# Attention's small matmuls in float32 as four tiles side by side, and the last weight's pages in the order of the products

## The chip, the cores and the metric

The kernel runs on one core of one Trainium2 chip. The metric is the device time of one execution in microseconds (us). The core has five engines that run their own instruction streams and wait for one another by semaphores: PE (TensorE, the matmuls, with its weight loads shown apart as PEld), DVE (VectorE), ACT (ScalarE), POOL (GpSimd) and SP (SyncE, which issues nearly all the DMAs here). Matmuls write PSUM, everything else lives in SBUF or DRAM.

## The reference

Attention over a small state, in both directions, and then two feed-forward blocks. All arrays are float32, except the four weight matrices, which arrive as float64.

```
x: [8, 8, 512, 64] (batch, head, position, 64)   state: [8, 8, 32, 64]
scores  = x @ state^T / 8        -> softmax over the 32 states   -> xread = a  @ state
scores2 = state @ x^T / 8        -> softmax over the 512 positions -> sread = a2 @ x
t = concat(xread, sread) as [4352 tokens, 512]
h = relu(t @ w_in)^2   @ w_out          (512 -> 2048 -> 512)
out = silu(h @ w2_in)  @ w2_out         (512 -> 2048 -> 512)
```

## The kernel before

**Precision.** The large matmuls are made of three products of one-pass float32 operands ("fp32r"): an operand is split into a high part (an ACT cast) and a low part (a subtraction on DVE or POOL), and high*high, high*low and low*high are summed in PSUM. A matmul on plain float32 operands shows as two MATMUL records and two LDWEIGHTS records in the trace.

**Attention.** It is done for a pair (b, g): batch b and a group g of four heads, so 16 pairs. `scores` fills one PSUM bank [4 heads x 32 states, 512 positions] from `x` (two halves l of 128 rows, two heads of 64 rows each). So that two heads of one half don't mix, the weights are a block form of the state, with zeros elsewhere. For the first three batches (b < NB = 3) the block form is a float32 quad `sblkf[b]`, filled by `s_put`, and each half is one float32 matmul of 128 rows, 128 columns and 512 moving columns. For the other five batches the block form (`sblk`, two pages, filled by `s_build`) and x (`x_split`) are split, and there are six one-pass matmuls. From the scores, DVE and ACT make both softmaxes. For the second direction `a2_T` transposes the softmax (four transposes on PE into PSUM), `a2_split` splits it on its way out of PSUM, `xn_split` splits x in its other layout, and `sread` makes 12 one-pass matmuls: 128 weight columns (4 heads x 32 states) against 256 moving columns (4 heads x 64), of which only the four diagonal blocks [32 x 64] are used; `sread_evac` takes those out. Scores, transposes and sread share the two PSUM banks `psD`.

**The first block.** `g_unit` multiplies the state with w_in once per batch pair (tile matmuls of 64 rows by 64 columns, with `tile_position`, weights from `st`, moving operand `cc`, into `psA` and `psB`). For batch j and each of 16 chunks c of the hidden width, `gemm1` multiplies the attention weights with that (6 matmuls into `psC`), `chain_a` takes relu and square, and `gemm2` adds the product with w_out (12 matmuls into `psA` and `psB`). The weights are converted from float64 on DVE and ACT as they come (`c_bits` and others).

**The second block.** Each of its two matmuls is done in Strassen-Winograd form with seven products. `gemm3(u, pp)` does token part u (five parts) and width part pp (four parts), in the order of products SEQ = 1, 2, 6, 7, 5, 3, 4; `gemm4(q)` does token part q (nine parts) in the order SEQ4 = 1, 6, 2, 7, 5, 4, 3. For w2_out there are 28 pages, w4p[jj][i] for width part jj and product i (256 KB each); product i of gemm4 needs those of all four jj, and its own operands `g0i0` and `g0i1` (two DMAs of 512 KB for token part 0, `g_op`). In the last token part of gemm3 `w4_load(pp)` asks for the seven pages of jj = pp, ahead of `gemm3(4, pp)`.

**Order.** Nothing is issued as it is written: `Plan` records all operations, with their reads and writes, and then a list scheduler orders each engine's stream. It always takes the operation that can start earliest by its cost model, and of those the most urgent. A `page` (50 buffers) or a `quad` (10 buffers) is given out in the order in which its first user was recorded; a later one may go first only if enough are free for all those ahead of it. DMAs are issued by SP in the planner's order. Two accumulating matmuls on the same PSUM region are dependent in the plan, and regions are told apart by partitions and bank. `cost` gives a matmul with a `tile_position` a quarter of its time.

Of the kernel before, what the change touches and what calls it, by code (L numbers as in the profile page):

```python
# [27 lines left out]
class Plan:  # L28
# [78 lines left out]
    def cost(self, eng, method, writes, reads, args):  # L107
        size = 1
        for ap in writes + reads:
            n = 1  # L110
            for d in ap.shape[1:]:
                n *= d
            size = max(size, n)
        psum = any(self.tiles.get(ap.tensor.name, (0, 0, ""))[2] == "ps" for ap in writes + reads)
        if eng == "dma":
            n = 1
            for d in writes[0].shape:
                n *= d
            return n * 4 / 360
        if eng == "pe":  # L120
            n = 1
            for d in writes[0].shape[1:]:
                n *= d
            if method == "transpose":
                return 109
            share = 4 if args.get("tile_position") else 1
            return max(n / 2.4 + 13, 109) * (4 if args["rhs"].dtype == F32 else 1) / share
        if eng == "act":
            return (145 if psum else 190) + size / 1.2 + (93 if "accum_out" in args else 0)
        if eng == "pool":  # L130
            return 190 + dict(tensor_tensor=2.2, memset=0.8).get(method, 3.5) * size
        fast = method in ("tensor_scalar", "tensor_copy", "memset") and not psum
        return 157 + size / (1.92 if fast else 0.96)
# [243 lines left out]
def attn_moe_moe_kernel(  # L377
# [52 lines left out]
    def page(name, dt=F32R):  # L430
        return plan.tile(pages, [P, 1024], dt, "page", name)
# [44 lines left out]
    def at(s, phase, fn, *a):  # L476
        ev[(s, phase)].append((fn, a))
# [78 lines left out]


    st = plan.tile(pages, [P, 4, 4, 2, NS], F32, "page", "st")
    sblk = [page(f"sblk{i}") for i in range(2)]
    sblkf = [quad(f"sblkf{b}") for b in range(NB)]  # L560
    ident = plan.tile(const, [P, P], F32, "ident", "ident")
    srT = plan.tile(pages, [P, 4, B * NS], F32, "page", "srT")

    def st_of(b, r):
        return st[r * 64:(r + 1) * 64, b // 2, :, b % 2].rearrange("p (g l) n -> p g l n", l=2)

    def s_build(b, dst, a):

        v = dst.rearrange("p (s g a c) -> p s g a c", s=2, g=2, a=4)
        for r in range(2):  # L570
            ps = slice(r * 64, (r + 1) * 64)
            src = st_of(b, r)
            hi, lo = (v[ps, s][:, :, a, r * NS:(r + 1) * NS] for s in range(2))
            split_into(hi, lo, src)

    def s_put(b, dst, a):

        v = dst.rearrange("p (g a c) -> p g a c", g=2, a=4)
        for r in range(2):
            ps = slice(r * 64, (r + 1) * 64)  # L580
            copy(v[ps, :, a, r * NS:(r + 1) * NS], st_of(b, r))


    w1p, gp = {}, {}
# [47 lines left out]

    a_x, a_xn, a_S, a_e, a_2, a_U, at_p = {}, {}, {}, {}, {}, {}, {}

    def sblk_build(b):
        s_build(b, sblk[b % 2], slice(0, 4, 3))

    def x_load(b, g):
        lo = page(f"xTr{b}{g}", F32)
        D.dma_start(lo.rearrange("p (l t) -> p l t", l=2),  # L640
                          xT[b, g * 256:(g + 1) * 256, :].rearrange("(l p) t -> p l t", p=P))
        a_x[(b, g)] = lo

    def x_split(b, g):
        raw, a_x[(b, g)] = a_x[(b, g)], (page(f"xThi{b}{g}"), page(f"xTlo{b}{g}"))
        split_into(*a_x[(b, g)], raw)

    def scores(b, g):
        x = a_x.pop((b, g))
        t = att_tile()  # L650
        a_S[(b, g)] = t
        if b < NB:
            for l in range(2):
                c0 = (2 * g + l) * P
                T.matmul(out=t, lhsT=sblkf[b][:, c0:c0 + P], rhs=x[:, l * 512:(l + 1) * 512],
                         start=l == 0, stop=l == 1)
            return
        hi, lo = x
        pg = sblk[b % 2]
        n = 0  # L660
        for l in range(2):
            c0 = (2 * g + l) * P
            for so, xp in ((0, hi), (512, hi), (0, lo)):
                T.matmul(out=t, lhsT=pg[:, so + c0:so + c0 + P], rhs=xp[:, l * 512:(l + 1) * 512],
                                 start=n == 0, stop=n == 5)
                n += 1

    def sm_first(b, g, defer=False):
        t = a_S[(b, g)]
# [59 lines left out]
            T.transpose(t[:, k * P:(k + 1) * P], e[:, k * P:(k + 1) * P], ident)  # L729
        a_2[(b, g)] = t  # L730

    def a2_split(b, g):
        t = a_2[(b, g)].rearrange("p (k c) -> p k c", k=4)
        pg = page(f"a2{b}{g}")
        v = pg.rearrange("p (k s c) -> p k s c", k=4, s=2)
        A.copy(v[:, :, 0, :], t)
        V.tensor_tensor(out=v[:, :, 1, :], in0=t, in1=v[:, :, 0, :].bitcast(F32), op=ALU.subtract)
        a_2[(b, g)] = v

    def xn_load(b, g):  # L740
        lo = page(f"xnr{b}{g}", F32)
# [1 line left out]
                      xN[b, :, g * 256:(g + 1) * 256].rearrange("(k p) c -> p k c", p=P))  # L743
        a_xn[(b, g)] = lo

    def xn_split(b, g):
        raw, a_xn[(b, g)] = a_xn[(b, g)], (page(f"xnhi{b}{g}"), page(f"xnlo{b}{g}"))
        split_into(*a_xn[(b, g)], raw)

    def sread(b, g):  # L750

        hi, lo = a_xn.pop((b, g))
        v = a_2.pop((b, g))
        t = att_tile()
        o = t[:, 0:256]
        for k in range(4):
            xs = slice(k * 256, (k + 1) * 256)
            for i, (w, x) in enumerate(((0, hi), (1, hi), (0, lo))):
                T.matmul(out=o, lhsT=v[:, k, w, :], rhs=x[:, xs], start=k + i == 0, stop=k == 3 and i == 2)
        a_2[(b, g)] = t  # L760

    def sread_evac(b, g):
        t = a_2.pop((b, g))
        for h in range(4):
            for e in range(2):
                ps = (h % 2) * 64 + e * NS
                V.transpose(out=srT[ps:ps + NS, 2 * g + h // 2, b * NS:(b + 1) * NS],
                            in_=t[h * NS:(h + 1) * NS, h * 64 + e * NS:h * 64 + (e + 1) * NS])


    gact, acc, yq, y_part = {}, {}, {}, {}
# [154 lines left out]
        v = pg.rearrange("p (k s c) -> p s k c", s=2, k=2)  # L926
        return v[:, 0], v[:, 1]

    def w4_load(jj):

        w4p[jj] = {}
        for i in SEQ4:
            w4p[jj][i] = page(f"w4{jj}_{i}")
            lo = f32(w4_views(w4p[jj][i])[1])
            if SRC_B[i] in (11, 12, 21, 22):
                w4_quarter(jj, SRC_B[i], lo)
            else:
                D.dma_start(lo, w4s_d[(SRC_B[i], jj)].rearrange("p (k c) -> p k c", k=2))

    def w4_split(jj, i):  # L940
        hi, lo = w4_views(w4p[jj][i])
        split_into(hi, lo, f32(lo))

    def x_op(u, i):
# [97 lines left out]
    def gemm4(q):  # L1042
# [4 lines left out]
        def prod(i, bank, first, last):  # L1047
            if q == 0:
                for jj in range(4):
                    w4_split(jj, i)  # L1050
            for b in range(c):
                for k in range(8):
                    hi, lo = gop[(q, i)][k // 4]
                    w = w4p[k // 2][i][:, k % 2 * 512:(k % 2 + 1) * 512]
                    ks = slice(k % 4 * c * P + b * P, k % 4 * c * P + (b + 1) * P)
                    for m, (g, o) in enumerate(((hi, 0), (hi, 256), (lo, 0))):
                        T.matmul(out=bank[:, b * 256:(b + 1) * 256], lhsT=g[:, ks], rhs=w[:, o:o + 256],
                                 start=first and b + k + m == 0, stop=last and k == 7 and m == 2,
                                 skip_group_check=True)
# [40 lines left out]

    def sched_attention(b, g, s, defer=False):
        at(s - 4, "dma", x_load, b, g)
        if b >= NB:
            if g == 0:
                at(s, "vec", sblk_build, b)
            at(s, "vec", x_split, b, g)
        elif g == 0:
            at(s, "vec", s_put, b, sblkf[b], slice(0, 4, 3))
        at(s + 1, "pe", scores, b, g)
        at(s + 1, "vec", sm_first, b, g, defer)  # L1110
        at(s + 2, "vec", sm1_exp, b, g)
        at(s + 3, "vec", sm1_norm, b, g)
        at(s + 4, "vec", sm1_T, b, g)
        if not defer:
            sched_sread(b, g, s + 4)

    def sched_sread(b, g, s):
        at(s - 3, "dma", xn_load, b, g)
        at(s, "vec", sm2_norm, b, g)
        at(s + 1, "pe", a2_T, b, g)  # L1120
        at(s + 1, "vec", a2_split, b, g)
        at(s + 1, "vec", xn_split, b, g)
        at(s + 2, "pe", sread, b, g)
        at(s + 2, "vec", sread_evac, b, g)

    def init():
        for t in sblkf:
            G.memset(t, 0.0)
        for t in sblk[::-1]:
            G.memset(t.bitcast(F32), 0.0)  # L1130

    def load_st():
        D.dma_start(st, sT)
# [7 lines left out]
    def slot(b, c):  # L1141
        return place[(b, c)]

    at(-14, "vec", init)
    for i in range(NC // 2):
        q, p = divmod(i, 2)
        if q < PARTS[0][1] // 4:
# [9 lines left out]
            at(-12, "dma", load_st)  # L1157
        at(n, "pe", g_unit, 2 * i)
        at(n, "pe", g_unit, 2 * i + 1)
    at(-10, "vec", s_put, 0, sblkf[0], slice(0, 4, 3))  # L1160
    for g in range(2):
        at(-8 + g, "dma", x_load, 0, g)
        at(-6 + g, "pe", scores, 0, g)
# [75 lines left out]
    for u in range(NU):  # L1239
        for pp in range(4):  # L1240
# [2 lines left out]
                w3_build(pp + 2)  # L1243
            if u == 1:
                w4_sums(pp)
            if u + 1 == NU:
                if pp == 3:
                    g_op(0, 1)
                w4_load(pp)
            gemm3(u, pp)  # L1250
            if pp == 3:
                for i in (SEQ if u + 1 < NU else SEQ4[1:]):
                    if u + 1 < NU:
# [45 lines left out]
```

## Time and profile before

| | |
|---|---|
| median of 3 runs | 1397.41 us (1393.69 to 1398.91) |
| profiled execution | 1396.56 us |
| its span, first to last instruction | 1394.8 us |
| PE busy | 1350.0 us, 97% |
| PE weight loads | 1169.2 us, 84% |
| DVE / ACT / POOL busy | 1006.7 (72%) / 693.0 (50%) / 44.8 us (3%) |
| mean granted TensorE clock | 0.991 of full speed |
| DMA | 283.19 MB, mean 203 GB/s |

The profiled execution is 1.8 us longer than its span. A share of busy time is a mean over stages: PE is idle for 45 us in all, nearly all of that in the first 135 us, around 1045 us and at the seams of the last stage.

### The profile page before, as it was taken

What the parts mean: (1) busy time and instruction counts of PE and PEld (TensorE: products, weight loads), DVE (VectorE), ACT (ScalarE), POOL (GpSimd) and SP (SyncE); (2) the same over time, 40 slices, a digit from 0 to 9 for tenths busy, and PEclk for the clock granted to TensorE, in tenths of its full rate; (3) what the DMA queues carried; (4) which work ended last, traced back from release to release, by engine and by line L of the source; (5) the groups of instructions that cost most, each with busy time, mean ns of one, the idle gap of its engine ahead of it and who ended that gap; (6) DMA issues with size and microseconds to landing.
All of it is one profiled execution on the core that took longest, in us unless ns stands there. A gap on an engine that the chain in (4) does not pass through costs nothing. (4 is left out here: it accounts for less than half of the span.)

```text
span 1394.8 us, 21037 instructions
## 1 busy us (share of the span) xinstructions
PE 1350.0 (97%) x7820; PEld 1169.2 (84%) x7820; DVE 1006.7 (72%) x1524; ACT 693.0 (50%) x1070; POOL 44.8 (3%) x42
## 2 busy tenths in 40 slices
PE   5889999999999999999999999999999999999998
PEld 1557688888888888888988889998879999999998
DVE  7898598878888888885997768677876455444443
ACT  6765776556555555554743424245563343333331
POOL 1000001100000000000020000000010000000000
PEclk9999999999999999999999999999999999999999
DMA  8841844535454535452759758678897566655664
GB/s 308 313 178 63 296 155 129 165 122 166 152 168 125 176 118 162 138 191 73 256 190 355 276 209 285 216 242 295 303 345 242 197 212 227 209 178 188 196 189 113
DMA packets 206965, 283.19 MB, mean 203 GB/s; under 512 B 13456, under 2 KB 148112, under 8 KB 206864
## 3 DMA queue, kind: packets, MB, share of 16 engines
q1 hardware_dynamic: 206864, 281.86, 60.7%
q8 instruction: 61, 1.00, 0.3%
q14 instruction: 40, 0.33, 0.1%
HBM read 161.35 MB, written 116.26 MB: 199 GB/s over the span
## 5 line engine op out<-in xcount | busy, mean ns | idle before, releaser
L185 ACT ACTIVATE rg<-psC 128x512 f32<-128x512 f32 (+1 forms) x144 | 82.6, 574 | 197.4 <-PE psC L185 195.4
L185 DVE TENSOR_TENSOR gact<-rg,gact 128x512 fp32r<-128x512 f32 (+1 forms) x139 | 90.8, 655 | 20.4 <-ACT rg L185 14.6
L185 PE MATMUL psC<-AThi,Ghi 128*128 128x512 f32 x256 | 100.9, 400 | 2.3 <-ACT rg L185 2.0
L185 PE MATMUL psC<-AThi,Glo 128*128 128x512 f32 x256 | 101.2, 401 | 1.6 <-DVE Glo L185 1.6
L185 PE MATMUL psC<-ATlo,Ghi 128*128 128x512 f32 x256 | 100.5, 397 | 1.9 <-DVE ATlo L185 1.9
L185 ACT ACTIVATE gact<-rg 128x512 fp32r<-128x512 f32 (+1 forms) x144 | 87.7, 609 | 7.6 <-DMA g<-go 4.1
L185 DVE TENSOR_TENSOR rg<-rg 128x512 f32<-128x512 f32 (+1 forms) x66 | 43.7, 662 | 50.5 <-ACT rg L185 50.3
L185 PEld LDWEIGHTS psC<-AThi,Ghi 128*128 128x128 f32 x256 | 48.1, 188 | 15.7 <-ACT rg L185 2.4
L185 PEld LDWEIGHTS psC<-AThi,Glo 128*128 128x128 f32 x256 | 48.2, 188 | 14.6 <-issue 2.1
L185 PEld LDWEIGHTS psC<-ATlo,Ghi 128*128 128x128 f32 x256 | 48.3, 189 | 13.8 <-DVE ATlo L185 2.6
L185 ACT ACTIVATE r<-r 128x1024 f32<-128x1024 f32 (+2 forms) x20 | 18.6, 932 | 62.9 <-DVE r L185 52.7
L185 DVE TENSOR_SCALAR cv<-cv 128x1024 f32<-128x1024 f32 (+1 forms) x64 | 43.3, 685 | 8.0 <-ACT cv L185 7.7
L185 ACT ACTIVATE rg<-rg 128x512 f32<-128x512 f32 (+1 forms) x78 | 46.3, 594 | 0.0
L185 ACT ACTIVATE cv<-raw 128x512 f32<-128x512 f32 x64 | 40.6, 667 | 7.3 <-DMA raw<-in_w_dram 6.3
L185 DVE SCALAR_TENSOR_TENSOR cc<-raw,cv 128x512 int32<-128x512 int32 x64 | 41.8, 683 | 3.3 <-DMA g<-go 3.1
L185 DVE SCALAR_TENSOR_TENSOR cv<-raw,cv 128x512 f32<-128x512 uint32 x64 | 41.6, 683 | 0.2
L185 DVE TENSOR_TENSOR W<-psC,U 128x512 f32<-128x512 f32 (+2 forms) x40 | 24.1, 609 | 22.5 <-PE psC L185 22.2
L185 PE MATMUL psA<-cc,st 64*64 64x512 f32 x128 | 26.1, 687 | 14.6 <-DVE cc L185 14.6
L185 DVE TENSOR_TENSOR Glo<-Glo,Ghi 128x1024 fp32r<-128x1024 f32 x31 | 37.7, 1215 | 1.2 <-ACT Ghi L185 1.0
L185 ACT ACTIVATE W<-W 128x1024 f32<-128x1024 f32 (+2 forms) x20 | 18.7, 933 | 39.6 <-DVE W L185 35.7
L185 ACT ACTIVATE r<-psA 128x512 f32<-128x512 f32 (+2 forms) x40 | 20.7, 534 | 33.3 <-PE psA L185 25.6
L185 ACT CAST Ghi<-Glo 128x1024 fp32r<-128x1024 f32 x32 | 33.5, 1045 | 1.2 <-DMA Glo<-go 1.2
(1244 smaller groups left out, 4587.2 us busy)
## 6 DMA issues: line engine op xcount, KB each, us to landing
raw<-in_w_dram SPq DMA_DIRECT2D x64, 512.0 KB, 6.2
t<-s SPq DMA_DIRECT2D x36, 512.0 KB, 5.1
Glo<-g SPq DMA_DIRECT2D x96, 128.0 KB, 4.3
t<-r SPq DMA_DIRECT2D x24, 512.0 KB, 4.5
xTr<-in_xT_dram SPq DMA_DIRECT2D x16, 512.0 KB, 7.6
g<-go SPq DMA_DIRECT2D x16, 512.0 KB, 5.2
xnr<-in_xN_dram SPq DMA_DIRECT2D x16, 512.0 KB, 5.2
x<-yt SPq DMA_DIRECT2D x32, 256.0 KB, 4.1
```

The source lines that it names most:

```text
L185: lambda engine=engine, method=method, a=a, k=k: getattr(engine, method)(*a, **k)))
```

## The change

Scores of all batches take the state `st` and the loaded `x` as they are, in float32, as four tile matmuls of 64 rows and 32 columns, one for each head, at tile positions (0,0), (64,32), (0,64) and (64,96). Sread takes x and one float32 copy of the transposed softmax, as 16 tile matmuls of 128 rows, 32 weight columns and 64 moving columns: four k steps, and in each the four heads at column positions 0, 32, 64 and 96. The block forms, their memsets and copies, and the splits of x, of the other layout of x and of the softmax go. The planner's cost of a tile matmul is divided by the share of the array that it takes. The pages of w2_out are asked for in the order of the products, seven behind each `gemm3(4, pp)`.

```diff
-            share = 4 if args.get("tile_position") else 1
+            share = 128 * 128 // (reads[0].shape[0] * writes[0].shape[0]) if args.get("tile_position") else 1
...
-    sblk = [page(f"sblk{i}") for i in range(2)]
-    sblkf = [quad(f"sblkf{b}") for b in range(NB)]
...
     def scores(b, g):
         x = a_x.pop((b, g))
         t = att_tile()
         a_S[(b, g)] = t
-        if b < NB:
-            for l in range(2):
-                c0 = (2 * g + l) * P
-                T.matmul(out=t, lhsT=sblkf[b][:, c0:c0 + P], rhs=x[:, l * 512:(l + 1) * 512],
-                         start=l == 0, stop=l == 1)
-            return
-        hi, lo = x
-        pg = sblk[b % 2]
-        n = 0
         for l in range(2):
-            c0 = (2 * g + l) * P
-            for so, xp in ((0, hi), (512, hi), (0, lo)):
-                T.matmul(out=t, lhsT=pg[:, so + c0:so + c0 + P], rhs=xp[:, l * 512:(l + 1) * 512],
-                                 start=n == 0, stop=n == 5)
-                n += 1
+            for r in range(2):
+                h, ps = 2 * l + r, slice(r * 64, (r + 1) * 64)
+                T.matmul(out=t[h * NS:(h + 1) * NS], lhsT=st[ps, b // 2, 2 * g + l, b % 2],
+                         rhs=x[ps, l * 512:(l + 1) * 512], start=True, stop=True, tile_position=(r * 64, h * NS))
...
-    def a2_split(b, g):
-        t = a_2[(b, g)].rearrange("p (k c) -> p k c", k=4)
-        pg = page(f"a2{b}{g}")
-        v = pg.rearrange("p (k s c) -> p k s c", k=4, s=2)
-        A.copy(v[:, :, 0, :], t)
-        V.tensor_tensor(out=v[:, :, 1, :], in0=t, in1=v[:, :, 0, :].bitcast(F32), op=ALU.subtract)
-        a_2[(b, g)] = v
+    def a2_copy(b, g):
+        c = quad(f"a2{b}{g}")
+        copy(c, a_2[(b, g)])
+        a_2[(b, g)] = c
...
     def sread(b, g):
...
+        x, a = a_xn.pop((b, g)), a_2.pop((b, g))
         t = att_tile()
-        o = t[:, 0:256]
         for k in range(4):
-            xs = slice(k * 256, (k + 1) * 256)
-            for i, (w, x) in enumerate(((0, hi), (1, hi), (0, lo))):
-                T.matmul(out=o, lhsT=v[:, k, w, :], rhs=x[:, xs], start=k + i == 0, stop=k == 3 and i == 2)
+            for h in range(4):
+                T.matmul(out=t[h * NS:(h + 1) * NS, 0:64], lhsT=a[:, k * P + h * NS:k * P + (h + 1) * NS],
+                         rhs=x[:, k * 256 + h * 64:k * 256 + (h + 1) * 64], start=k == 0, stop=k == 3,
+                         tile_position=(0, h * NS))
...
-            if u + 1 == NU:
-                if pp == 3:
-                    g_op(0, 1)
-                w4_load(pp)
-            gemm3(u, pp)
+            if u + 1 == NU and pp == 3:
+                g_op(0, 1)
+            gemm3(u, pp)
+            if u + 1 == NU:
+                for i, jj in [(i, jj) for i in SEQ4 for jj in range(4)][7 * pp:7 * pp + 7]:
+                    w4_load(i, jj)
```

Also gone are `s_build`, `s_put`, `x_split`, `xn_split`, their places in the schedule, and `init` with its five memsets on POOL. `w4_load` now asks for one page.

## Rows read from the trace of the kernel before

**Rows 1.** By stretch: length, busy PE, PEld, DVE, ACT, POOL; clock, DMA share, GB/s.
```profile
15.00:45.00 30.00, 27.64 (x141) 7.74 (x134) 26.41 (x45) 22.65 (x43) 0.00 (x0) 0.94 0.84 284
45.00:75.00 30.00, 26.62 (x108) 19.74 (x106) 23.20 (x33) 21.80 (x36) 0.00 (x0) 1.00 0.94 343
75.00:135.00 60.00, 51.86 (x202) 40.01 (x203) 58.31 (x96) 31.68 (x57) 0.92 (x2) 0.91 0.28 103
...
160.00:700.00 540.00, 540.00 (x2676) 456.50 (x2675) 448.80 (x791) 317.11 (x534) 19.18 (x16) 1.00 0.49 157
...
1000.00:1030.00 30.00, 30.00 (x137) 24.66 (x136) 23.89 (x31) 14.91 (x23) 4.75 (x3) 1.00 0.99 331
...
1050.00:1060.00 10.00, 10.00 (x71) 10.00 (x71) 6.24 (x6) 3.19 (x4) 0.00 (x0) 0.80 0.78 276
```

**Rows 2.** Attention's matmuls on PE by form: count, busy us, mean ns of one.
```profile
L185 PE MATMUL psD<-xnhi,a 128*128 128x256 f32 x128 | 32.9, 280 | 0.0
...
L185 PE MATMUL psD<-xThi,sblk 128*128 128x512 f32 x40 | 15.7, 392 | 0.0
L185 PE MATMUL psD<-xTr,sblkf 128*128 128x512 f32 x24 | 13.2, 639 | 3.7 <-issue 2.4 <-ACT Sc L185 1.3
```

**Rows 3.** PE in order of time at 210 us, scores of a later batch.
```profile
210.77 0.39 PE L185 MATMUL psD<-xThi,sblk 128*128 128x512 f32 x1
211.00 0.39 PE L185 MATMUL psB<-gact,hi('w2', 6)_464 128*128 128x512 f32 x1
```

**Rows 4.** Busy time over 17 spacings between one-pass matmuls of sread.
```profile
233.83:235.86 2.04, 2.04 (x18) 1.00 0.31 100
```

**Rows 5.** PE in order of time at 23 us: 64x64 tiles around a full float32 matmul.
```profile
23.70 1.09 PE L185 MATMUL psA<-cc,st 64*64 64x512 f32 x8
24.61 1.04 PE L185 MATMUL psB<-cc,st 64*64 64x512 f32 x8
25.57 1.12 PE L185 MATMUL psD<-xTr,sblkf 128*128 128x512 f32 x2
26.63 1.09 PE L185 MATMUL psA<-cc,st 64*64 64x512 f32 x8
```

**Rows 6.** The weight loads of the same stretch, in order of time.
```profile
27.11 0.15 PEld L185 LDWEIGHTS psB<-cc,st 64*64 64x64 f32 x4 [0.28 <-issue]
27.54 0.15 PEld L185 LDWEIGHTS psB<-cc,st 64*64 64x64 f32 x4 [0.28 <-issue]
```

**Rows 7.** PE in order of time at 151 us: a full one-pass matmul among tiles.
```profile
151.45 0.50 PE L185 MATMUL psC<-AThi,Ghi 128*128 128x512 f32 x1
151.88 0.65 PE L185 MATMUL psB<-cc,st 64*64 64x512 f32 x2
```

**Rows 8.** PE in order of time at 229 us: transposes.
```profile
228.80 0.82 PE L185 MATMUL psD<-ident,e 128*128 128x128 f32 x6
...
229.70 0.27 PE L185 MATMUL psD<-ident,e 128*128 128x128 f32 x1
```

**Rows 9.** PE in order of time at 1045 us: the seam between gemm3 and gemm4.
```profile
1044.85 0.50 PE L185 MATMUL psC<-w,g050hi 128*128 128x256 f32 x2 [1.75 <-ACT g050hi L185]
1048.89 0.58 PE L185 MATMUL psD<-w,g070lo 128*128 128x256 f32 x1 [3.54 <-DVE g070lo L185]
```

**Rows 10.** SP's queue in order of time ahead of that seam.
```profile
1023.87 2.12 SPq L185 DMA_DIRECT2D w<-w4d  x2
1026.04 0.49 SPq L185 DMA_DIRECT2D g060lo<-t  x1
...
1034.31 1.41 SPq L185 DMA_DIRECT2D g050lo<-t  x1
```

**Rows 11.** A page of w2_out as a DMA: size, us to landing.
```profile
w<-w4s SPq DMA_DIRECT2D x16, 256.0 KB, 4.7
```

**Rows 12.** The splits of x for sread on ACT and DVE, ns min/median/max.
```profile
L185 ACT CAST xnhi<-xnr x16: 1032/1038/1064, 220.6 to 545.1; 128x1024 fp32r<-128x1024 f32 x16
L185 DVE TENSOR_TENSOR xnlo<-xnr,xnhi x16: 1159/1218/1226, 226.6 to 551.2; 128x1024 fp32r<-128x1024 f32 x16
```

More of the change, by code (lines that the diff above doesn't have):

```diff
@@ L558, in attn_moe_moe_kernel @@
     st = plan.tile(pages, [P, 4, 4, 2, NS], F32, "page", "st")
-    sblk = [page(f"sblk{i}") for i in range(2)]
-    sblkf = [quad(f"sblkf{b}") for b in range(NB)]
     ident = plan.tile(const, [P, P], F32, "ident", "ident")
     srT = plan.tile(pages, [P, 4, B * NS], F32, "page", "srT")
[L564 to L581, printed above, removed]
     w1p, gp = {}, {}
@@ L633, in attn_moe_moe_kernel @@
     a_x, a_xn, a_S, a_e, a_2, a_U, at_p = {}, {}, {}, {}, {}, {}, {}
-    def sblk_build(b):
-        s_build(b, sblk[b % 2], slice(0, 4, 3))
     def x_load(b, g):
@@ L642, in x_load @@
         a_x[(b, g)] = lo
-    def x_split(b, g):
-        raw, a_x[(b, g)] = a_x[(b, g)], (page(f"xThi{b}{g}"), page(f"xTlo{b}{g}"))
-        split_into(*a_x[(b, g)], raw)
     def scores(b, g):
@@ L744, in xn_load @@
         a_xn[(b, g)] = lo
-    def xn_split(b, g):
-        raw, a_xn[(b, g)] = a_xn[(b, g)], (page(f"xnhi{b}{g}"), page(f"xnlo{b}{g}"))
-        split_into(*a_xn[(b, g)], raw)
     def sread(b, g):
-        hi, lo = a_xn.pop((b, g))
-        v = a_2.pop((b, g))
+        x, a = a_xn.pop((b, g)), a_2.pop((b, g))
         t = att_tile()
-        o = t[:, 0:256]
         for k in range(4):
-            xs = slice(k * 256, (k + 1) * 256)
-            for i, (w, x) in enumerate(((0, hi), (1, hi), (0, lo))):
-                T.matmul(out=o, lhsT=v[:, k, w, :], rhs=x[:, xs], start=k + i == 0, stop=k == 3 and i == 2)
+            for h in range(4):
+                T.matmul(out=t[h * NS:(h + 1) * NS, 0:64], lhsT=a[:, k * P + h * NS:k * P + (h + 1) * NS],
+                         rhs=x[:, k * 256 + h * 64:k * 256 + (h + 1) * 64], start=k == 0, stop=k == 3,
+                         tile_position=(0, h * NS))
         a_2[(b, g)] = t
@@ L767, in sread_evac @@
                 V.transpose(out=srT[ps:ps + NS, 2 * g + h // 2, b * NS:(b + 1) * NS],
-                            in_=t[h * NS:(h + 1) * NS, h * 64 + e * NS:h * 64 + (e + 1) * NS])
+                            in_=t[h * NS:(h + 1) * NS, e * NS:(e + 1) * NS])
     gact, acc, yq, y_part = {}, {}, {}, {}
@@ L927, in w4_views, with w4_load @@
         return v[:, 0], v[:, 1]
[L929 to L938, printed above, removed]
+    def w4_load(i, jj):
+        w4p[(jj, i)] = page(f"w4{jj}_{i}")
+        lo = f32(w4_views(w4p[(jj, i)])[1])
+        if SRC_B[i] in (11, 12, 21, 22):
+            w4_quarter(jj, SRC_B[i], lo)
+        else:
+            D.dma_start(lo, w4s_d[(SRC_B[i], jj)].rearrange("p (k c) -> p k c", k=2))
     def w4_split(jj, i):
-        hi, lo = w4_views(w4p[jj][i])
+        hi, lo = w4_views(w4p[(jj, i)])
         split_into(hi, lo, f32(lo))
@@ L1053, in prod @@
                     hi, lo = gop[(q, i)][k // 4]
-                    w = w4p[k // 2][i][:, k % 2 * 512:(k % 2 + 1) * 512]
+                    w = w4p[(k // 2, i)][:, k % 2 * 512:(k % 2 + 1) * 512]
                     ks = slice(k % 4 * c * P + b * P, k % 4 * c * P + (b + 1) * P)
@@ L1102, in sched_attention @@
         at(s - 4, "dma", x_load, b, g)
[L1103 to L1108, printed above, removed]
         at(s + 1, "pe", scores, b, g)
@@ L1120, in sched_sread @@
         at(s + 1, "pe", a2_T, b, g)
-        at(s + 1, "vec", a2_split, b, g)
-        at(s + 1, "vec", xn_split, b, g)
+        at(s + 1, "vec", a2_copy, b, g)
         at(s + 2, "pe", sread, b, g)
         at(s + 2, "vec", sread_evac, b, g)
[L1126 to L1130, printed above, removed]
     def load_st():
@@ L1142, in slot @@
         return place[(b, c)]
-    at(-14, "vec", init)
     for i in range(NC // 2):
@@ L1159, in attn_moe_moe_kernel @@
         at(n, "pe", g_unit, 2 * i + 1)
-    at(-10, "vec", s_put, 0, sblkf[0], slice(0, 4, 3))
     for g in range(2):
```

## The prediction

> **What bounds the kernel now.** I read the busy time by stretch first, then PE's groups by form, then PE in order of time wherever an operation of the change stands or has a relative, and last the queue of SP ahead of the one seam that the change moves. The reader is to see two things in the stretches [rows 1]. From 160 to 700 us, where nearly all of the attention sits, PE is busy for 540.00 of 540 us at the full granted clock, so there only PE time counts: an ACT cast or a DVE subtraction that goes is worth nothing. Before 135 us PE is not full: it lacks 2.4 us of 30, 3.4 of 30 and 8.1 of 60, and DVE (26.4 of 30 and 58.3 of 60 us) or the DMA engines (share 0.94 in the middle stretch) are the fuller ones. PE time saved there is mostly turned into waiting for them. "Busy" also says nothing of how dense the matmuls stand; that is read from start to start: a one-pass matmul of 512 columns takes 0.23 us [rows 3], one of 256 columns 2.04 / 17 = 0.120 us [rows 4].
>
> **Sread.** Before: 12 one-pass matmuls of 256 columns, 12 x 0.120 = 1.44 us for a pair, 16 pairs, 23.0 us (their count fits the 128 records with the high part of x, two thirds of 192 [rows 2]). After: 16 float32 tile matmuls of 64 columns. No row shows tiles over 128 rows, nor 32 columns wide. The nearest relative are the 64x64 tiles of g_unit, on float32 too. There four tiles start as one: their four weight loads stand in one row of 0.15 us in all, and the next four come 0.43 us later [rows 6], so a wave of four tiles of 512 columns, half of a float32 matmul each, takes 0.43 us. It is no more than half of the 1.06 us that one full float32 matmul of two records takes with its way in [rows 5], so four tiles cost what one matmul costs. With 64 columns a wave would be 0.43 / 8 = 0.054 us, and sread has 4 k steps x 2 halves = 8 waves: 0.43 us.
>
> To that comes the change of tiling. From tiles to a full matmul: two waves and the way out take 0.96 us where 2 x 0.43 = 0.86 are the waves, so 0.10 [rows 5]. From a full one-pass matmul into tiles: 0.43 us from its start where 0.23 would do, so 0.20 [rows 3, 7], and the first two waves after a full matmul take 0.91 instead of 0.86, another 0.05 [rows 5]. Together 0.35 us for each burst of tiles that stands among full matmuls. In the plan the 16 matmuls stay together: the four heads write different partitions, so they aren't dependent on each other, and k + 1 of a head comes three matmuls after k. That makes 0.43 + 0.35 = 0.78 us, the lower bound. From above: if tiles over the same 128 rows run one after the other, each matmul costs at least the shortest spacing that the trace has between untiled matmuls, that of the transposes, (0.82 - 0.27) / 5 = 0.11 us [rows 8], and with 32 records 3.5 + 0.35 = 3.9 us. Between them lies that the tiles run together but their short waves don't cover the weight loads: 8 x (0.15 + 0.054) + 0.35 = 2.0 us [rows 6]. I take 0.9 us, near the lower end, since the only tiles in the trace behave so, with 0.12 us for weight loads seen between the waves. Gain 16 x (1.44 - 0.9) = 8.6 us; bounds +10.6 us and -39 us.
>
> A rule of the Trainium skill speaks against this part: "TensorEngine Tiling (Array Packing)", Instruction Overhead, gives each matmul some 60 cycles whatever its size and advises not to take the tiling from a dimension that is already small, as sread's 64 columns are. As an estimate by that page, with the overhead paid in series, 32 records x 60 cycles at 2.4 GHz are 0.8 us more for a pair, 1.6 us in all, and the gain of this part would turn into a loss of 2.6 us; it is a milder form of rival 1 below. The rows on four weight loads that start within one record of 0.15 us [rows 6] don't show such a series for tiles, but their waves are eight times as long.
>
> **Scores.** For batches 3 to 7 (10 pairs) before: six one-pass matmuls of 0.23 us, 1.36 us; they stand between other matmuls of the same size, at no extra cost [rows 3]. After: four tiles of 512 columns in float32, two waves, 0.86 + 0.35 = 1.21 us. Two of the four share the same 64 rows at different columns, as two of g_unit's do. Gain 10 x 0.15 = 1.5 us. From above, if only the two row halves overlap, 1.72 + 0.35 = 2.07 us, a loss of 7 us; I take the first, since g_unit's waves hold two tiles in the same rows. For batches 0 to 2 (6 pairs) before: two full float32 matmuls (24 records [rows 2]), each alone among tiles 1.06 + 0.10 + 0.05 = 1.21 us, 2.4 us for a pair; after, 1.04 us if half of the change of tiling is due between 64x64 and 64x32. That is 6 x 1.4 = 8 us of PE, but in the stretches where DVE and DMA set the pace [rows 1]. I count 1 us, bounds 0 and 8.
>
> **What goes from the other engines.** Each split of x for sread is a cast of 1.04 us on ACT and a subtraction of 1.22 us on DVE [rows 12], 16 times, with 10 like them for the scores and 16 of half the size on the way out of PSUM. That is some 40 us of DVE and 30 us of ACT, all between 160 and 700 us but for little, under a PE that never waits there [rows 1]: nothing. If that cover were gone, the softmax chains on DVE (448.8 of 540 us busy) would be next, and they get lighter. The memsets on POOL and the copies of the block form lie ahead of or beside the first weight conversion; nothing.
>
> **The pages of w2_out.** No bytes are added; 28 DMAs of 256 KB (two of 128 KB for some) change places. At the seam PE waits 1.75 us for `g050hi` and 3.54 us for `g070lo` [rows 9], and the granted clock is 0.80 over the ten us behind it, at two levels of 2.4 and 1.2 GHz some 4 us at the lower one, 2 us lost [rows 1]: 7 us. What is late are g06 to g05: they are issued from 1026.04 to 1034.31 us, only after the last weight page at 1023.87 [rows 10], while the DMA engines are full (share 0.99, 331 GB/s [rows 1]). In the old order the last seven pages are those of jj = 3 for every product. In the new one they are those of products 4 and 3, due last, and the planner may then put g06, g02 and g07 ahead of them if page buffers are free. 7 x 256 KB [rows 11] at 331 GB/s are 5.5 us by which those could come earlier. Against it, each seven pages are now asked for behind the temporaries of their gemm3, seven page buffers later, so weight loads that ran before move into the full stretch: again up to 7 pages, 5.5 us later. SP's stores of gemm3's results, in the same queue, keep their place. Bounds: -7 us (seam gone) and +6 us with the same clock loss. I take a gain of 3 us, since what moves behind is due last and what moves ahead is what PE waits for.
>
> **Sum.** 1396.56 - 8.6 - 1.5 - 1 - 3 = 1382.5 us, against the profiled execution, which lies 0.85 us under the median; rounded, 1382.
>
> **Rivals.**
> 1. Short tiles don't cover their weight loads: sread 2.0 us, 16 x 0.56 = 9 us lost instead of 8.6 won. For it: eight times less streaming for each load than in any tile row. Against: the second set of loads of g_unit starts while the first tiles stream. Time 1396.56 + 9 - 5.5 = 1400. The section Part 3 of "TensorE: Matmul & The Clock Gate" in the Trainium skill states that loads overlap with running matmuls only where the row groups differ; here all four tiles take all rows.
> 2. The other side: tiles over all 128 rows don't overlap at all. Sread 3.9 us, 16 x 2.46 = 39 us lost; 1396.56 + 39 - 5.5 = 1430. It decides from 1.78 us for an sread on (1.44 + 5.5 / 16). For it: no row has four tiles in the same rows. Against: g_unit has two.
> 3. The seam gets longer: 6 us lost instead of 3 won, the rest as forecast: 1382.5 + 9 = 1391.5. For it: a full DMA stretch into which seven more pages move. Against: they are needed 20 us later than what passes them.
> 4. Nothing of it can be seen because PE wasn't the limit of the stage: the trace says otherwise for 160 to 700 us; 1396.
>
> **How the numbers follow.** Chances: the forecast 0.68, rival 1 0.08, rival 2 0.07, rival 3 0.12, rival 4 0.05. The forecast's own range is 1369 (sread 0.78, the early 8 us, the seam gone) to 1391 (sread 1.2, no early gain, no change at the seam). The range takes in rivals 3 and 4 to 1397 and leaves out rivals 1 and 2 and a rest below. Half a per cent, 7 us, is what a measurement of this kernel tells from no change: faster means under 1390.4. The forecast gives 0.66 for that, rival 3 0.06; within lie the rest of these, rival 4 and most of rival 1, 0.19; slower are rival 2 and a little of rival 1, 0.09.
>
> **What would show it.** The 16 tile matmuls of a pair start within some 0.6 us of each other, and the next full matmul 0.9 us after the first (right), or their starts are 0.05 us or more apart in every record (rivals 1 and 2). Scores: four records start as one, then four more 0.43 us later. From 160 us on the same chunk of the first block is reached earlier pair by pair, by 0.5 to 0.8 us for each. DVE's sum falls by some 40 us with nothing to show for it. At the seam the first `g06` is issued before the last weight pages, and PE's two waits shrink. The prediction is wrong if tile bursts are broken up by other matmuls (0.35 us for each break), if the planner's new costs (four scores tiles at about half their time, sread at twice) reorder the first 135 us for the worse, or if the seam opens.

## The result, and the profile after

The changed kernel takes 1402.92 us (median of 7, 1398.95 to 1406.27) where the kernel before took 1397.41 (7 runs beside it): ratio 1.0052, interval 1.0035 to 1.007. It is about 5 us slower; 1382 was forecast, within 1369 to 1397. The profiled execution of the changed kernel (1398.95 us, span 1397.1) is the fastest of its seven, so the traces show 2.3 of these 5 us.

Where they are is read from places that both kernels reach: the last matmul of `g_unit` (`cc`), the first and last `gemm1` of the attention (`AThi`), the last matmul of gemm3 (`x43`) and the first of the second token part of gemm4 (`g110`). A trace's view by tile gives each group's first and last start. Of the changed kernel (durations min/median/max in ns, then first and last start in us):

```profile
L186 PE MATMUL psB<-cc,st x128: 589/589/1057, 17.0 to 157.0; 64*64 64x512 f32 x128
...
L186 PE MATMUL psC<-AThi,Ghi x256: 388/389/682, 48.4 to 658.1; 128*128 128x512 f32 x128
...
L186 PE MATMUL psC<-x43hi,w x32: 389/389/389, 981.0 to 1041.7; 128*128 128x512 f32 x32
...
L186 PE MATMUL psA<-w,g110hi x16: 283/283/283, 1075.0 to 1088.0; 128*128 128x256 f32 x16
```

And the same groups of the kernel before:

```profile
L185 PE MATMUL psB<-cc,st x128: 589/589/1111, 16.4 to 154.1; 64*64 64x512 f32 x128
...
L185 PE MATMUL psC<-AThi,Ghi x256: 387/389/796, 45.2 to 645.3; 128*128 128x512 f32 x128
...
L185 PE MATMUL psC<-x43hi,w x32: 389/389/403, 971.2 to 1031.1; 128*128 128x512 f32 x32
...
L185 PE MATMUL psA<-w,g110hi x16: 283/283/283, 1072.3 to 1082.1; 128*128 128x256 f32 x16
```

| stretch, us | before | changed | difference |
|---|---|---|---|
| up to the last `cc` | 154.1 | 157.0 | +2.9 |
| attention: from there to the last `AThi` | 491.2 | 501.1 | **+9.9** |
| to the last `x43` | 385.8 | 383.6 | -2.2 |
| seam: to the first `g110` | 41.2 | 33.3 | **-7.9** |
| to the end of the span | 322.5 | 322.1 | -0.4 |

So the seam closed, by more than forecast, and the attention, where 10 us should have been won, lost as much. Attention's matmuls by form in the changed kernel, with the wait that ended the idle time before them (columns as in [rows 2]):

```profile
L186 PE MATMUL psD<-xTr,st 64*32 64x512 f32 x128 | 26.9, 600 | 0.8 <-ACT Sc L186 0.8
L186 PE MATMUL psD<-xnr,a 128*32 128x64 f32 x512 | 18.7, 223 | 5.1 <-DVE srT L186 5.1
```

A wait of 5.1 us for DVE that the kernel before did not have, and far more busy time than 16 bursts of 0.9 us. PE in order of time shows why. First the scores of one pair, then sread of another, in the changed kernel:

```profile
305.00 1.04 PE L186 MATMUL psD<-xTr,st 64*32 64x512 f32 x2
305.97 0.33 PE L186 MATMUL psD<-ident,e 128*128 128x128 f32 x1
306.23 1.04 PE L186 MATMUL psD<-xTr,st 64*32 64x512 f32 x2
307.20 0.33 PE L186 MATMUL psD<-ident,e 128*128 128x128 f32 x1
...
331.18 0.30 PE L186 MATMUL psD<-xnr,a 128*32 128x64 f32 x2
331.41 0.49 PE L186 MATMUL psB<-gact,lo('w2', 2)_323 128*128 128x512 f32 x1
331.83 0.30 PE L186 MATMUL psD<-xnr,a 128*32 128x64 f32 x2
332.06 0.49 PE L186 MATMUL psB<-gact,hi('w2', 2)_322 128*128 128x512 f32 x1
332.49 0.63 PE L186 MATMUL psD<-xnr,a 128*32 128x64 f32 x26
333.42 0.30 PE L186 MATMUL psD<-xnr,a 128*32 128x64 f32 x2 [0.30 <-DVE srT L186]
```

The tiles don't stay together. Two of sread's matmuls (two records each) stand alone, each between full matmuls of gemm2; and of the scores of this pair each tile stands alone between transposes. A lone sread tile with its neighbour takes 331.83 - 331.18 = 0.65 us; 0.23 are the neighbour's, so 0.42 us for one tile, where the first run below does 16 in 0.58. A lone score tile takes 0.97 us to the start of the next matmul; four together take 0.99 there. Counted in order of time, the trace has 36 sread bursts, 22 of them lone tiles, where 16 pairs need 16, and 24 bursts of scores, 14 of them in the attention's stretch, where 10 would do. And the last tile waits for DVE, which reads the block of head 0 out of the same bank while head 3 is still being multiplied.

PE waits for DVE like this eight times, 5.1 us in all. The longest wait, 1.73 us, has a second cost. Shortly behind it the granted clock falls to its lower level, 1.2 GHz, from 554.5 to 557.9 us, and the one-pass matmuls there stand 0.43 us apart instead of 0.23. Eight of them are 1.6 us; the kernel before keeps the full clock in this stretch. Not every such wait is followed by a fall: one of 1.55 us at 281.9 us isn't. PE in order of time, then the columns of [rows 1]:

```profile
553.38 0.30 PE L186 MATMUL psD<-xnr,a 128*32 128x64 f32 x2 [1.73 <-DVE srT L186]
...
555.22 0.63 PE L186 MATMUL psA<-gact,hi('w2', 2)_322 128*128 128x512 f32 x1
555.64 0.63 PE L186 MATMUL psC<-AThi,Ghi 128*128 128x512 f32 x1
```

```profile
554.00:558.00 4.00, 4.00 (x12) 3.17 (x11) 1.23 (x6) 0.00 (x0) 0.00 (x0) 0.57 1.01 258
```

### The profile page after: what moved, and what is told of

It is laid out like the page before. It is cut to its first block, busy times and chain, and to the rows that moved or that the text cites. A ratio compares the mean times of both kernels' runs of the same rounds, so it can differ in the third digit from the quotient of the medians.

```text
span 1397.1 us, 21649 instructions
## 1 busy us (share of the span) xinstructions
PE 1351.2 (97%) x8184; PEld 1143.3 (82%) x8184; DVE 972.0 (70%) x1482; ACT 666.1 (48%) x1030; POOL 34.2 (2%) x25
## 5 line engine op out<-in xcount | busy, mean ns | idle before, releaser
L186 DVE TENSOR_TENSOR gact<-rg,gact 128x512 fp32r<-128x512 f32 (+1 forms) x144 | 96.7, 673 | 29.6 <-ACT rg L186 25.9
L186 PE MATMUL psC<-AThi,Ghi 128*128 128x512 f32 x256 | 105.0, 413 | 3.9 <-ACT rg L186 2.2
L186 DVE STREAM_TRANSPOSE srT<-psD 32x32 f32<-32x32 f32 x128 | 27.2, 213 | 11.0 <-PE psD L186 9.3
L186 DVE TENSOR_TENSOR U<-psB,U 128x512 f32<-128x512 f32 (+2 forms) x40 | 23.9, 606 | 14.8 <-PE psB L186 12.5
```

The costliest lines, as they stand in the source:

```text
L186: lambda engine=engine, method=method, a=a, k=k: getattr(engine, method)(*a, **k)))
```

## The experiments

The theory after this reading, A: the tiles are as fast as forecast, and the loss is in the broken bursts. Against it B: the tiles, or the two PSUM banks, are slow by themselves; C: the planner's new cost line misplaces the work; D: the gain at the seam does not come from the order of the pages. The attention stretch below is that of the table above, read from one trace for each run. The runs were made in five sessions, each beside the kernel before, so across sessions the ratios are to be compared.

| run | median, us | ratio to before (interval) | attention stretch, us |
|---|---|---|---|
| changed kernel | 1402.92 | 1.0052 (1.0035 to 1.007) | 501.1 |
| both bursts whole | 1375.17 | 0.9858 (0.9825 to 0.9891) | 478.3 |
| the same, planner told real costs | 1378.82 | 0.9886 (0.9855 to 0.9918) | 478.3 |
| page order alone | 1390.74 | 0.9964 (0.9948 to 0.9981) | 491.2 |
| attention's part alone | 1407.65 | 1.0089 (1.0064 to 1.0115) | 501.2 |
| only scores whole | 1391.74 | 0.997 (0.9953 to 0.9986) | 498.6 |
| only sread whole | 1392.51 | 0.9975 (0.996 to 0.9991) | 490.8 |
| both whole, a full matmul inside sread | 1383.31 | 0.9905 (0.9879 to 0.9932) | 486.6 |
| both whole, the same matmul behind sread | 1378.91 | 0.988 (0.9857 to 0.9904) | 482.4 |
| both whole, unused splits | 1375.26 | 0.9842 (0.9812 to 0.9872) | 478.3 |
| both whole, g_unit's tiles too | 1374.90 | 0.9834 (0.9804 to 0.9863) | 473.3 (last `cc` only at 158.9) |
| changed kernel, old tile cost | 1397.42 | 0.9999 (0.9982 to 1.0016) | 500.2 |
| both whole, old page order | 1380.84 | 0.9883 (0.9857 to 0.9909) | 478.3 |
| changed kernel, no gap in the plan | 1393.28 | 0.9984 (0.9968 to 1.0001) | 484.3 |
| kernel before, no gap in the plan | 1399.86 | 1.0031 (1.0014 to 1.0048) | 489.5 |

**Both bursts whole.** `plan.together` records several matmuls as one operation of the planner:

```diff
+SCORES_NS, SREAD_NS = 452.0, 1744.0
...
-                T.matmul(out=t[h * NS:(h + 1) * NS], ..., tile_position=(r * 64, h * NS))
+                tiles.append(dict(out=t[h * NS:(h + 1) * NS], ..., tile_position=(r * 64, h * NS)))
+        plan.together(T, SCORES_NS, tiles)    # sread likewise: 16 tiles, SREAD_NS
```

> The changed kernel, but the four score tiles of a pair, and the 16 sread tiles of a pair, are each one operation of the planner, which nothing can be put between (its costs kept, 452 and 1744 ns). Theory A (broken bursts: 36 separate bursts of sread tiles and 24 of score tiles, where 16 and 16 would do, each with a change of tiling in and out): the stretch from the first gemm1 of batch 3 to the last gemm1 of the attention, 478 us in the changed kernel and 468 before, falls to about 463, and the time to about 1388 us. Theory B (the tiles themselves, or waits for the two PSUM banks of the attention, cost the time): the stretch stays within 3 us of 478, the time within 4 us of 1403.

1375.17 us: by the ratios 27 us under the changed kernel, and 20 under the one before. That is 13 us less than theory A had said. The table's stretch fell from 501.1 to 478.3, by 22.8 us (the 478 of the expectation belong to a shorter stretch of the changed kernel, from the first gemm1 of batch 3). Theory B is out. In this trace sread and scores stand whole, and nothing waits for `srT`:

```profile
L193 PE MATMUL psD<-xnr,a 128*32 128x64 f32 x512 | 10.3, 222 | 0.0
L193 PE MATMUL psD<-xTr,st 64*32 64x512 f32 x128 | 16.8, 600 | 1.6 <-ACT Sc L197 1.6
```

The lines are the groups by form; below, PE in order of time.

```profile
330.02 0.39 PE L197 MATMUL psB<-gact,lo('w2', 3)_341 128*128 128x512 f32 x1
330.34 1.06 PE L193 MATMUL psD<-xTr,st 64*32 64x512 f32 x8
331.33 0.50 PE L197 MATMUL psB<-gact,hi('w2', 3)_340 128*128 128x512 f32 x1
...
351.68 0.61 PE L197 MATMUL psB<-gact,hi('w2', 6)_459 128*128 128x512 f32 x2
352.23 0.65 PE L193 MATMUL psD<-xnr,a 128*32 128x64 f32 x32
352.81 0.50 PE L197 MATMUL psB<-gact,lo('w2', 6)_460 128*128 128x512 f32 x1
353.15 0.40 PE L197 MATMUL psC<-AThi,Ghi 128*128 128x512 f32 x1
```

Sread's 32 records take 0.58 us from start to next start; with the two one-pass matmuls before them at 0.23 each, the way in is 352.23 - 351.68 - 0.46 = 0.09, and the next full one stands 0.34 us instead of 0.23 before its successor (352.81 to 353.15), 0.11 more: 0.78 us, the lower bound of the prediction. Scores take 0.99 and the same 0.2: 1.2 us, as forecast.

**With real costs.**

```diff
-SCORES_NS, SREAD_NS = 452.0, 1744.0
+SCORES_NS, SREAD_NS = 1200.0, 800.0
```

> As the run with bursts kept together, but the planner is told 1200 ns for a burst of score tiles and 800 for one of sread, about what the changed kernel's trace shows, in place of 452 and 1744. Theory A: what counts is that bursts are whole, so within 4 us of that run, about 1388. Theory C (the planner's wrong costs misplace the work): at least 5 us faster than that run, and the start of the first gemm1, 3 us later in the changed kernel than before, comes back.

1378.82 us and the same stretch to the tenth. The costs are not what counts for the attention; the 4 us lie ahead of it (last `cc` at 156.3 instead of 152.6 us).

**The parts of the change.** Page order alone, and everything but the page order:

> The kernel before with the order of the pages of the last weight alone. Theory A (the 9 us that the changed kernel wins back at the seam between gemm3 and gemm4 come from this order): about 1388 us, PE's waits of 1.75 and 3.54 us at the seam gone. Theory D (the seam closed because the attention before it was late, or by chance of the plan): within 3 us of 1397.

> The changed kernel with the old order of the last weight's pages, so the attention's part of the change alone. Theory A: the attention loses some 13 us up to its end and the seam gives nothing back, about 1411 us. Theory D: about 1403 us, as the changed kernel.

1390.74 and 1407.65 us, beside 1394.86 for the kernel before in the same session: 4 us won and 13 lost, both some 3 us short of what theory A had said, and clear of theory D. PE's waits around the seam in the kernel with the page order alone (1000 to 1060 us) are one, and in the kernel with the attention's part alone (990 to 1080 us) the old ones are there [rows 9]:

```profile
PE psA L185 <- ACT u L185: 0.6, 1, 0.6
```

```profile
PE psD L186 <- DVE g070lo L186: 3.4, 1, 3.4
PE psC L186 <- ACT g050hi L186: 1.8, 1, 1.8
```

That the waits follow the page order and not the attention's lateness decides against D. SP's queue with the page order alone: `g060` and `g061` now go ahead of the last weight pages (in [rows 10] behind them).

```profile
1024.33 0.43 SPq L185 DMA_DIRECT2D g060lo<-t  x1
1024.80 1.17 SPq L185 DMA_DIRECT2D w<-w4d  x2
1026.07 0.38 SPq L185 DMA_DIRECT2D g061lo<-t  x1
1027.01 1.51 SPq L185 DMA_DIRECT2D w<-w4d  x3
```

**One burst whole, the other not.**

> The changed kernel with only the four score tiles of a pair kept together; sread's 16 stay single operations of the plan. Theory A (each break costs, wherever it stands): nine score bursts fewer, at about 1.2 us each, but five of them early where PE waits anyway, so 5 to 9 us, about 1396. Theory F (sread's breaks are all of the loss): 1403 and no change.

> The changed kernel with only sread's 16 tiles kept together. Theory A: 22 single tiles at 0.45 us (0.23 of their own, 0.25 for the way into tiles) and the 5.1 us in which PE waited for sread_evac inside a burst go, 12 to 15 us, about 1389. Theory G (it is the scores alone): 1403.

1391.74 and 1392.51 us, 11 and 10 less than the changed kernel; neither F nor G, both matter. The first gained more than expected: its last `cc` starts at 150.7 us instead of 157.0, so whole score bursts pay early too. In the attention stretch the two savings, 2.5 and 10.3 us, are together only 12.8 of 22.8. The trace with sread whole shows most of the rest: there a score tile is broken off for every pair of the stretch, in 21 bursts instead of the changed kernel's 14.

```profile
339.41 1.04 PE L197 MATMUL psD<-xTr,st 64*32 64x512 f32 x2
340.38 0.50 PE L197 MATMUL psB<-gact,hi('w2', 3)_340 128*128 128x512 f32 x1
340.82 1.05 PE L197 MATMUL psD<-xTr,st 64*32 64x512 f32 x6
341.80 0.50 PE L197 MATMUL psC<-AThi,Ghi 128*128 128x512 f32 x1
```

One tile, a full matmul, then the other three: 2.39 us to the next full matmul, where 0.99 for four tiles and 0.23 would do, so 1.17 us lost, and in this trace score tiles keep PE busy for 34.2 us instead of 16.8. Seven bursts more at that price are 8.2 of the missing 10.0 us. With the scores whole it goes the other way, if less: 24 lone sread tiles instead of 22, and the granted clock falls twice in the stretch (at 274.9 and 544.5 us, beside waits of 1.55 and 1.73 us for DVE) instead of once. Mending one kind of burst moves the break to the other.

**The price of one break.** The same full-array float32 matmul of 64 columns, into columns of the bank that nobody reads, in the middle of each sread burst or behind it:

```diff
+            if k == 1:                        # in the control: behind the loop
+                tiles.append(dict(out=t[:, 64:128], lhsT=a[:, 0:P], rhs=x[:, 0:64], start=False, ...))
```

> The kernel with both bursts kept together (first run), with one full-array float32 matmul of 64 columns put into the middle of each sread burst; it writes 64 unused columns of the bank, nothing else changes. To be compared with the next run, where the same matmul stands behind the burst. Theory A: a break costs a way out and a way in, 0.35 us, so this run is 16 x 0.35 = 5.6 us slower than the next. Theory B (breaks are free, the loss of the changed kernel is something else): the two are within 2 us.

> As the run before, with the extra matmul behind the 16 tiles of the burst, where the change of tiling is due anyway. Both theories: 16 times its own 0.15 to 0.3 us slower than the kernel without it, 1378 to 1380 us.

1383.31 and 1378.91 us. The first line is a burst with the matmul inside, the next full matmul behind it; then the control:

```profile
357.29 1.16 PE L193 MATMUL psD<-xnr,a 128*32 128x64 f32 x34
358.38 0.50 PE L197 MATMUL psB<-gact,lo('w2', 6)_460 128*128 128x512 f32 x1
```

```profile
353.46 1.02 PE L193 MATMUL psD<-xnr,a 128*32 128x64 f32 x34
354.29 0.48 PE L197 MATMUL psB<-gact,lo('w2', 6)_460 128*128 128x512 f32 x1
```

1.09 against 0.83 us: a break costs 0.26 us, and 16 of them 4.2 us in the stretches, 4.4 in the medians. The prediction had 0.35, and the expectation 5.6 us.

**Work on other engines.** The 16 splits of x for sread put back, into pages that nobody reads:

> The kernel with both bursts kept together, plus the 16 splits of x for sread that the change removed (a cast of 1.04 us on ACT and a subtraction of 1.22 us on DVE or twice that on POOL each), into pages that nobody reads. The prediction counted the removal of such work as nothing, since PE never waits there. If so: within 2 us of 1375. Theory H (the relief of DVE and ACT and of the page buffers is part of the gain): 5 us or more slower.

1375.26 us, and the same stretch, with DVE busy 389.4 us instead of 370.1 from 160 to 630 us (the columns of [rows 1]; this kernel first, then the one with both bursts whole). Theory H is out for these splits; the other operations that went were not put back.

```profile
160.00:630.00 470.00, 470.00 (x2588) 375.24 (x2587) 389.36 (x704) 266.93 (x435) 4.40 (x3) 1.00 0.50 157
```

```profile
160.00:630.00 470.00, 470.00 (x2587) 375.26 (x2586) 370.11 (x682) 253.12 (x423) 10.58 (x6) 1.00 0.50 157
```

**Three more runs.** The four tiles of a g_unit step as one operation; the old cost of a tile in the changed kernel; both bursts whole with the old page order:

> The kernel with both bursts kept together, and the four 64x64 tiles of each step of g_unit too, at 904 ns. If broken bursts matter there as well: a few us less before the first gemm1 and around 150 us, 1371 to 1374. If these stretches wait for DVE anyway: 1375 within 2 us.

> The changed kernel with the planner's old cost of a tile matmul (a quarter of its time whatever its size). Theory A (the bursts break because each tile is an operation by itself): the plan breaks them as before (36 sread bursts, 24 of scores), 1403 within 4 us. Theory C (the new cost line breaks them): 1390 or less.

> The kernel with both bursts kept together, but the old order of the last weight's pages. If the two parts of the change are independent: slower than 1375 by what the order alone gave (4 us by the medians, 7 us by the traces), 1379 to 1382. If the seam's gain hangs on when the attention ends: 1375 or over 1385.

1374.90: g_unit's breaks cost nothing that can be seen; its last tiles only move within the stream. 1397.42: the cost line does not break the bursts (stretch 500.2), so C fails for the attention. Yet without it the kernel is 5.5 us faster by the medians and 7 by the ratios, outside the 4 us that theory A had allowed. The two profiled executions differ by only 1.2 us; the first gemm1 is 2.9 us earlier there, 45.5 us instead of 48.4, and the rest was not located. 1380.84: the page order is worth 3.5 us by the ratios and 5.7 by the medians to the kernel with whole bursts, so the two parts are about independent.

**What breaks them.** In the plan, two matmuls that add to the same PSUM region stand 3 ns apart. Behind each of gemm2's last matmuls, which add to one bank, the planner's next start for gemm2 is 3 ns off, and it takes what can start now, which can be one tile of attention. That is the pattern above, a lone tile, gemm2 on `psB`, a lone tile, gemm2 on `psB`.

```diff
-                   pe=dict(act=197, dve=196, pool=200, pe=3, dma=0),
+                   pe=dict(act=197, dve=196, pool=200, pe=0, dma=0),
```

> The changed kernel with one number of the planner changed: the time it sees between two dependent matmuls is 0 instead of 3 ns. Theory J (those 3 ns behind each accumulating matmul of gemm2 let the planner slip one tile of attention into the gap, so this number broke the bursts): in the plan the sread bursts are whole (14 bursts for 16 pairs) and the score tiles nearly so, and the time comes within 4 us of the kernel with both bursts kept together, 1375 to 1379. Theory K (the gain of that kernel came from something else in how a burst is planned as one operation): above 1390.

> Control: the kernel before with the same number at 0. It has full matmuls only in the attention, between which no tiling changes. Theory J: within 3 us of 1397. If the 3 ns cost something by themselves: faster by 5 us or more, and the run before this one has to be judged against that.

1393.28 and 1399.86 us. Theory J's time was missed by 14 us, and by the time alone theory K's mark was met. In the attention stretch theory J holds: 484.3 us, 16.8 less than the changed kernel, and there all bursts of sread and scores are whole in the trace. Of the 6.0 us that are still missing against the operation as a whole, 4.5 are the waits for DVE inside bursts:

```profile
PE psD L186 <- DVE srT L186: 4.5, 9, 1.5
```

Elsewhere the number costs time by itself: the last `cc` starts at 160.7 us here and at 161.2 in the control, 7 us later than in the kernel before, and both wait 9.6 and 9.7 us for `u` in gemm4. Judged by its control, 0.9984 against 1.0031, the same edit takes 10 us from the changed kernel and gives 4 to the other. So the gap is shown to be what breaks the bursts of the stretch; that it accounts for all 27 us of the first run is not shown.

The control also shows that the gap was at work before. In the kernel before, the 60 one-pass score matmuls stand in 60 places and sread's 192 in 152; in the control they stand in 10 and 14, whole. The stretch is 1.7 us shorter for it, 489.5 instead of 491.2.

## Why the prediction was wrong

**The step that failed** is in the part on sread: "In the plan the 16 matmuls stay together: the four heads write different partitions, so they aren't dependent on each other". That is true of the tiles among themselves. But the full matmuls around them do depend on each other, and each such dependency leaves a gap in the plan into which one tile can be put. Nothing that the prediction read says that the scores' four tiles stay together either; the sum has it so. The interleaving of scores with gemm matmuls, one by one [rows 3], was this very thing at work in the kernel before, as the control shows: nearly harmless there (at most 1.7 us), since no tiling changes between full matmuls. I took from it the spacing and not the rule. Broken bursts were named as what would make the prediction wrong, with 0.35 us for each, but stand neither in the sum nor among the rivals. The measured time lies near rival 1's 1400 us by chance; its mechanism, weight loads that aren't covered, did not come.

With the measured prices: 22 lone sread tiles at 0.42 us are 9.2 us, the waits for DVE 5.1, four score bursts too many in the stretch at 1.17 are 4.7, and the lower clock behind one of the waits 1.6; together 20.6 of the 22.8 us between the changed kernel and the one with whole bursts. The last 2 us were not located.

**The steps that held,** each in the kernel that keeps bursts whole:
- Sread, 1.44 to 0.9 us (bounds 0.78 and 3.9): 0.78. Tiles over all 128 rows do run four at a time, and their weight loads are covered; rivals 1 and 2 fall. The 60 cycles for each matmul that the Trainium skill states ("TensorEngine Tiling (Array Packing)", Instruction Overhead) don't add up for tiles side by side: 32 records in 0.58 us are 18 ns each, less than 25 ns for 60 cycles at 2.4 GHz, their streaming included. Nor does the rule of the Trainium skill that weight loads overlap with running matmuls only across row groups ("TensorE: Matmul & The Clock Gate", Part 3) show here as a cost: all these tiles take all rows.
- Scores, 1.21 us: 1.2.
- Both together, 8.6 + 1.5 = 10.1 us, or 12.1 with sread at its measured 0.78: the stretch is 12.9 us shorter than before.
- Splits, casts and memsets at nothing: the 16 splits of x for sread, put back, cost nothing; the others were not put back.
- A change of tiling, 0.35 us both ways: 0.26 inside a burst.

**Sizes that were off.** The early stretch should have given 1 us and took 2.9 in the trace. Most of that goes with the score bursts: in the six runs that keep them whole, under the same costs and with g_unit as it was, the last `cc` starts at 150.7 to 153.1 us (154.1 in the kernel before); in the three that break them, under the new cost line, at 157.0 to 157.9. With the old cost line it starts at 155.4; that line was named as a danger and priced at nothing. The seam was put at 3 us of 7: it gave 7.9 in the trace of the changed kernel, 4 to 6 in the medians. PE's waits of 1.75 and 3.54 us are gone, and the granted clock stays at 1.00 through the changed kernel's seam, 1042 to 1075 us, where the kernel before had 0.80 behind its waits [rows 1]:

```profile
1050.00:1060.00 10.00, 10.00 (x85) 10.00 (x85) 9.18 (x9) 5.61 (x6) 0.00 (x0) 1.00 1.07 392
1060.00:1070.00 10.00, 10.00 (x86) 10.00 (x85) 5.66 (x7) 3.62 (x5) 0.00 (x0) 1.00 1.09 383
```

The direction rested on the right mechanism, as rival 3 did not come.

**What stays open:** some 3 us of the 5 by which the changed kernel's median is above that of before, since its profiled execution was the fastest of seven; how much of the new cost line's 5 to 7 us is more than a plan that happens to come out worse ahead of the attention; and why the plan without the gap loses elsewhere what it does.

## What to carry to other kernels

Matmuls that are to run side by side on the array are worth their price only as a block: give the scheduler the block as one operation, or a lone tile can cost as much as the whole group, as a score tile does here, or half of it, as in sread. When matmuls of another tiling come into a stream that a scheduler interleaves freely, price the change of tiling for every place where it may interleave, and read from the trace before whether it does. And split a change into its parts before judging it: here one half was worth 4 to 6 us and the other lost 13, for a reason that a few lines of the planner mend. A broken group also lets another engine in between, and the waits that follow can cost clock on top of their own length.

## What the runs showed of the hardware

Eight waves of four float32 tiles of 128 rows, 32 columns and 64 moving columns take 0.58 us with the way out, within 0.15 us of 8 x 0.054, an estimate of their streaming from the 0.43 us of a 64x64 wave of 512 columns [rows 6]. A lone float32 tile of 64 rows, 32 columns and 512 moving columns takes 0.97 us with the way out, as long as four side by side (0.99). A change of tiling in the middle of such a burst costs 0.26 us.
